# Block-sparse attention with a feed-forward stage: the values of the two end blocks as wide products

## The chip, the core and the metric

The kernel runs on one core of one Trainium2 chip. The core has a matrix engine (TensorE, called PE in the profile; its weight loads are listed apart as PEld), a vector engine (VectorE, DVE), an engine for activation functions (ScalarE, ACT), a general one (GpSimd, POOL) and one that issues transfers (SyncE, SP). Each follows its own list of instructions in order; they wait for one another through semaphores. Matrix products read SBUF and write PSUM. The metric is the time of one execution on the device in microseconds (us). Less is better.

## The reference

The first half is attention for 4 batches and 8 heads, 768 tokens, head size 64. Tokens form 24 blocks of 32. A query block sees itself and its two neighbours, the first and the last block, and three blocks drawn for it; the first and last query blocks see everything. The second half is a feed-forward layer on the 3072 tokens with 512 features, 2048 hidden.

```python
mask = np.abs(blk_i - blk_j) <= window          # window = 1, in blocks of 32
mask = mask | (blk_i == 0) | (blk_j == 0) | (blk_i == n_blocks - 1) | (blk_j == n_blocks - 1)
for qb in range(n_blocks):
    for kb in sampled_blocks[qb]:
        mask[qb * block:(qb + 1) * block, kb * block:(kb + 1) * block] = True
scores = np.where(mask, scale * q @ k.T, -1e9)
attn = softmax(scores);  x = attn @ v           # all heads of a token side by side
out = (gelu(x @ w_in)) @ w_out                  # exact gelu (erf)
```

## The kernel before

The tokens are worked on in nine units of two or three groups (`units`). A group ("quad") is four query blocks, 128 tokens; the first and the last group of a batch have three, because the end query blocks 0 and 23 see everything and are done apart, in "d" rounds. The other groups are made of "s" rounds of two query blocks (one in the second round of a three-block group).

For each s round the kernel does these steps, with the line numbers of the profile:

- `scores` (L305, tile `sc`): products of the queries with eight key blocks for each query block: block 0, the three neighbours, the three drawn ones, block 23. Four heads lie on the four partition quarters, two sets of four heads (G) side by side. Weights are 64 rows by 32 columns.
- `maxima` (L330, tile `nm`, DVE): the negative maximum of each row.
- `exponentials` (L342, tile `pp`, ACT): one exponential of 256 columns for each query block and G. It stores two key blocks interleaved, so that pairs of bf16 can be turned as one 32-bit word. Before the change the blocks 2c and 2c+1 are interleaved.
- `turned` (L359, tile `pT`, DVE): transposes 32x32 words, so that keys lie on partitions. `ptpool` has six such tiles, one for each round.
- `values` (L407, tile `av`), called twice for a group, once for each G ("half"): for each of the eight key blocks c, each query block s and each row half h it makes one product. Weights are the probabilities (64 rows by 32 columns), the moving operand is V with a column of ones, 2 x 65 = 130 columns. The output of query block s goes to partitions 32s to 32s+31, that of row half h to one of two banks.
- `divided` (L422 to L426, DVE) divides by the sum; `outputs` (L436 on PE, tile `tx`, and L444 on ACT, tile `xT`) turns the result for the feed-forward stage.

Where block 0 or 23 is also a neighbour of the query block, it would be counted twice. `values` then takes V from block NB of `kv`, which holds zeros in all its columns, the column of ones included. The same block stands in for drawn blocks that occur twice.

The d rounds use `ptd` (L363) and their values (L383) have weights of 64 x 64.

The feed-forward stage of a unit has `ffn1_step` (L457, tile `hp`, then the gelu of L460) and `ffn2_pieces` (L479, tile `op`), products with 128x128 weights. The order of work is written out by hand (`manual_schedule`): after the first layer of unit n comes `attention` of unit n+1, whose rounds overlap one another, and between their steps PE gets a given number (`quota`) of products of the second layer of unit n as filler. The values of a group are put into PE's list some rounds after the group's last scores, when `due` says so. `psV`, the PSUM pool of `av`, has one buffer.

The lines around the change:

```python
for c in range(8):
    for s, (rnd, i, j) in enumerate(slots):
        ...
        for h in range(2):
            rows = slice(64 * h, 64 * h + 64)
            nc.tensor.matmul(av[32 * s:32 * s + 32, h, V2 * G:V2 * G + V2],
                             lhsT=pv[rows, c // 2, :, c % 2], rhs=src[rows],
                             start=(c == 0), stop=(c == 7))
```

Of the kernel before, what the change touches and what calls it, by code (L numbers as in the profile page):

```python
# [9 lines left out]
F32 = mybir.dt.float32  # L10
BF16 = mybir.dt.bfloat16
I32 = mybir.dt.int32
AF = mybir.ActivationFunctionType
# [6 lines left out]
def kernel(  # L20
# [10 lines left out]
    nc = tc.nc  # L31
    P = 128
    B, H, S, D = q.shape
    assert (B, H, S, D) == (4, 8, 768, 64)
    BL = 32
    NB = S // BL
# [6 lines left out]
    V2 = 2 * VW  # L43
# [13 lines left out]
    ctx.enter_context(tc.manual_schedule())  # L57
    const = ctx.enter_context(tc.tile_pool(name="const", bufs=1))
    ppool = ctx.enter_context(tc.tile_pool(name="ppool", bufs=3))
    ptpool = ctx.enter_context(tc.tile_pool(name="ptpool", bufs=6))  # L60
    small = ctx.enter_context(tc.tile_pool(name="small", bufs=4))
    opool = ctx.enter_context(tc.tile_pool(name="opool", bufs=3))
    psA = ctx.enter_context(tc.tile_pool(name="psA", bufs=2, space=PSUM))
# [17 lines left out]
    g = const.tile([P, KOUT, UT], BF16, name="g")  # L81
# [12 lines left out]
    def sampled(i, r):  # L94
        c0 = GW * (i // 3) + 4 * BW + DW * (i % 3) + BW * r
        return gb[:, c0:c0 + BW]
# [176 lines left out]
    class Unit:  # L273
        def __init__(self, b, quads, dense, i0=0):
# [6 lines left out]
            for grp in self.groups:  # L281
# [4 lines left out]
    units = [Unit(0, (1,), True, 9), Unit(0, (2, 0), False), Unit(0, (3, 4, 5), False)]  # L286
    units += [Unit(b, quads, dense) for b in range(1, B)
              for quads, dense in (((1, 2, 0), True), ((3, 4, 5), False))]
    column = {}
    for n, unit in enumerate(units):  # L290
        for t, quad in enumerate(unit.quads):
# [3 lines left out]
    st = {}  # L295
# [41 lines left out]
    def exponentials(rnd):  # L337
        A, nm = st.pop((rnd, "A")), st.pop((rnd, "nm"))
        pp = ppool.tile([P, 1024], BF16, name="pp")

        def one(dst, src, bias):
            nc.scalar.activation(dst.rearrange("p (c k e) -> p c e k", e=2, k=BL),  # L342
                                 src.rearrange("p (c e k) -> p c e k", e=2, k=BL),
                                 AF.Exp, bias=bias)
        if rnd[0] == "s":
            n = len(rnd[1])
            for x in range(2 * n):
                a = 512 * (x // n) + 256 * (x % n)
                one(pp[:, 256 * x:256 * x + 256], A[:, a:a + 256], nm[:, x:x + 1])
        else:  # L350
            one(pp[:, 0:S], A[:, 0:S], nm[:, 0:1])
        st[rnd, "pp"] = pp

    def turned(rnd):
        pp = st.pop((rnd, "pp"))
        if rnd[0] == "s":
            w = 512 * len(rnd[1])
            pt = ptpool.tile([P, 1024], BF16, name="pT")
            nc.vector.transpose(pt[:, 0:w].bitcast(F32), pp[:, 0:w].bitcast(F32))  # L359
            st[rnd, "pt"] = pt  # L360
        else:
            _, x, G = rnd
            nc.vector.transpose(  # L363
                ptd[:, G].rearrange("p c x q e -> p c (x q e)").bitcast(F32)[:, :, BL * x:BL * x + BL],
                pp[:, 0:S].bitcast(F32).rearrange("p (c k) -> p c k", k=BL))
# [5 lines left out]
    def values(unit, grp, half):  # L371
        kv = kvs[unit.b % 2]
        if half == 0:
            st[grp, "av"] = psV.tile([P, 2, 512], F32, name="av", tag="V")
        av = st[grp, "av"]
        if grp[0][0] == "d":
            pv = ptd.rearrange("p g c x q e -> p g c (x q) e")
            for c in range(NB // 2 * half, NB // 2 * (half + 1)):
                for G in range(2):
                    for h in range(2):  # L380
                        rows = slice(64 * h, 64 * h + 64)
                        c0 = KC + V2 * G
                        nc.tensor.matmul(av[64 * G:64 * G + 64, h, 0:V2],  # L383
                                         lhsT=pv[rows, G, c // 2, :, c % 2],
                                         rhs=kv[rows, c, c0:c0 + V2],
                                         start=(c == 0), stop=(c == NB - 1))
            n, m = 4, 2
        else:
            slots = [(rnd, i, j) for rnd in grp for i, j in enumerate(rnd[1])]
            G = half  # L390
            c0 = KC + V2 * G
            for c in range(8):
                for s, (rnd, i, j) in enumerate(slots):
                    x = len(rnd[1]) * G + i
                    pv = st[rnd, "pt"][:, 256 * x:256 * x + 256]
                    pv = pv.rearrange("p (c k e) -> p c k e", k=BL, e=2)
                    if c in (0, 7):
                        blk = 0 if c == 0 else NB - 1
                        blk = NB if abs(blk - j) <= 1 else blk
                        src = kv[:, blk, c0:c0 + V2]  # L400
                    elif c < 4:
                        src = kv[:, j - 2 + c, c0:c0 + V2]
                    else:
                        src = sampled(unit.place[j], c - 4)[:, c0:c0 + V2]
                    for h in range(2):
                        rows = slice(64 * h, 64 * h + 64)
                        nc.tensor.matmul(av[32 * s:32 * s + 32, h, V2 * G:V2 * G + V2],  # L407
                                         lhsT=pv[rows, c // 2, :, c % 2], rhs=src[rows],
                                         start=(c == 0), stop=(c == 7))
            n, m = len(slots), 4  # L410
            if half:
                for rnd in grp:
                    st.pop((rnd, "pt"))
        if half:
            st[grp, "av"] = av, n, m

# [87 lines left out]
    def attention(unit, filler, quota, tail, held=0, hooks=None, late=False, ahead=None):  # L504
# [17 lines left out]
        def weigh():  # L522
            _, grp, half = due.pop(0)
            values(unit, grp, half)
            if half:
                weighed.append(grp)
# [4 lines left out]
        for it in range(-1, n):  # L531
            last = it + 1 == n
            if not last:
                scores(*rounds[it + 1])
            else:
                while due and due[0][0] <= it:
                    weigh()
            ready = len(given)
            if weighed and not last:
                divide()  # L540
            if it >= 1:
                turned(rounds[it - 1][1])
            if weighed and last:
                divide()
            if not last:
                maxima(rounds[it + 1][1])
            if it >= 0:
                exponentials(rounds[it][1])
            store_finished()
            for f in hooks.get(it, ()):  # L550
                f()
            fill(quota[it + 1])
            if not late:
                store_finished()
            if ready:
                outputs(unit, given.pop(0))
            while not last and due and due[0][0] <= it:
                weigh()
        if not ahead:
            table(AF.Gelu)  # L560
        turned(rounds[n - 1][1])
        for m in tail[:-1]:
            fill(m)
# [54 lines left out]
    for n, unit in enumerate(units):  # L618
        nxt = units[n + 1] if n + 1 < len(units) else None
        b = unit.b  # L620
        fresh = nxt is not None and nxt.b != b
# [91 lines left out]
```

## Time and profile before

| | |
|---|---|
| time, median of 3 runs | 307.44 us (307.2 to 308.11) |
| profiled execution: its time / its span | 308.78 us / 307.0 us |
| busy: PE, PEld, DVE, ACT, POOL | 255.3, 150.1, 219.7, 207.6, 107.9 us |
| value products of s rounds (L407) | 2816, of 218 to 225 ns median each (overlapping) |
| chain that ended last | PE 53%, ACT 17%, DVE 13%, issue 7%, DMA 6% |
| mean granted TensorE clock | 0.972 |

How to read it: a product's duration runs from its start to its modelled end, and products overlap; what one costs in a stream is the distance between starts. Groups are listed as line, engine, operation, output from inputs, shape of the weights (rows * columns), shape of the moving operand, count, then busy time, mean length of one, and the idle time before them with what ended it. In the timeline the first column is the start in us, the second the length; a bracket is idle time before it and what ended it. The chain is followed back from the last instruction to what released each step.

### The profile page before, as it was taken

The page shows a single profiled execution, that of the slowest core. Times are in us where ns is not written, and L with a number is a line of the kernel's source. Part 1 is how long each engine was busy: PE and PEld are TensorE (multiplying, and loading weights), DVE is VectorE, ACT ScalarE, POOL GpSimd, SP SyncE. Part 2 cuts the span into 40 slices and gives each one's busy share as a digit, 9 for nine tenths or more (in the row PEclk, how much of TensorE's full clock was granted, in tenths as well). Part 3 has the DMA queues.
Part 4 walks back from the last instruction along what each step waited for, and adds up shares of the span by engine and source line. Part 5 has one row for each costly group of instructions (what it writes and reads, how often), then busy time and mean ns, then how long its engine had stood idle before and what let it go on. Part 6 is the DMA issues. An engine that isn't in the chain of part 4 may idle for free.

```text
span 307.0 us, 12104 instructions
## 1 busy us (share of the span) xinstructions
PE 255.3 (83%) x5191; PEld 150.1 (49%) x5240; DVE 219.7 (72%) x505; ACT 207.6 (68%) x383; POOL 107.9 (35%) x191
## 2 busy tenths in 40 slices
PE   1656894897589898988799879989998899889994
PEld 0514743653255454534455445635553566355643
DVE  6388675869599895978499876979977979583000
ACT  9666385387476885589367875699668866885621
POOL 8658679987257000567074000500030005000000
PEclk9999996699799999999799999999999999999999
DMA  7999999999949011999699001901000111011001
GB/s 106 157 106 207 207 175 153 210 92 135 116 36 106 3 40 38 190 94 164 75 81 59 15 32 52 204 18 72 5 36 0 38 38 38 0 48 59 3 36 70
DMA packets 90633, 25.44 MB, mean 83 GB/s; under 512 B 81745, under 2 KB 87634, under 8 KB 90578
## 3 DMA queue, kind: packets, MB, share of 16 engines
q0 software_dynamic: 68352, 13.64, 80.8%
q1 hardware_dynamic: 22226, 11.01, 14.3%
q8 instruction: 41, 0.67, 1.0%
q14 instruction: 14, 0.11, 0.2%
HBM read 27.26 MB, written 6.29 MB: 109 GB/s over the span
## 4 chain that ended last, share of the span: by engine, by line
PE 53%; ACT 17%; DVE 13%; issue 7%; DMA 6%; POOL 1%; DVEq 1%; ACTq 0%; POOLq 0%
PE hp L457 24%; PE op L479 12%; PE av L407 9%; ACT pp L342 8%; DVE nm L330 5%; ACT L369 4%; DMA w_in_sb<-in_moe_w_in_dram 3%; ACT g L460 3%; DMA kv<-in_v_dram 2%; PE sc L305 2%; DVE pT L359 2%; PE tx L436 2%; PE av L500 2%; PE op L500 2%; DVE gb L269 2%
## 5 line engine op out<-in xcount | busy, mean ns | idle before, releaser
L342 ACT ACTIVATE pp<-sc,nm 128x256 bf16<-128x256 f32 (+1 forms) x192 | 92.0, 586 | 17.6 <-DVE nm L330 9.2
L457 PE MATMUL hp<-xT,w_in_sb 128*128 128x384 bf16 (+2 forms) x576 | 89.3, 319 | 1.7 <-ACT xT L444 1.3
L479 PE MATMUL op<-w_out_sb,g 128*128 128x512 bf16 x288 | 76.3, 383 | 4.8 <-issue 3.7
L460 ACT ACTIVATE g<-hp 128x768 bf16<-128x768 f32 (+4 forms) x81 | 53.5, 675 | 34.4 <-PE hp L457 34.4
L457 PEld LDWEIGHTS <-w_in_sb 128*128 128x128 bf16 x576 | 56.9, 103 | 34.5 <-issue 4.1
L269 POOL COPY gb<-kv 128x388 bf16 (+1 forms) x69 | 33.3, 530 | 109.0 <-DVE gb L260 83.0
L330 DVE TENSOR_REDUCE nm<-sc 128x4 f32<-128x1024 f32 (+1 forms) x48 | 53.0, 1107 | 7.1 <-PE sc L305 7.0
L269 DVE COPY gb<-kv 128x388 bf16 (+1 forms) x195 | 54.3, 358 | 0.1
L479 PEld LDWEIGHTS <-g 128*128 128x128 bf16 x336 | 28.7, 98 | 36.0 <-issue 12.3
L407 PE MATMUL av<-kv,pT 64*32 64x130 bf16 x1760 | 34.7, 231 | 11.0 <-issue 4.3
L407 PEld LDWEIGHTS <-pT 64*32 64x32 bf16 x2816 | 28.8, 95 | 27.8 <-issue 12.8
L359 DVE STREAM_TRANSPOSE pT<-pp 128x512 f32<-128x512 f32 (+1 forms) x48 | 31.5, 656 | 6.7 <-ACT pp L342 4.5
L444 ACT COPY xT<-tx 128x192 bf16<-128x192 bf16 (+2 forms) x33 | 13.6, 442 | 24.6 <-PE tx L436 24.5
L305 PE MATMUL sc<-gb,qT 64*32 64x256 bf16 x704 | 19.7, 279 | 9.2 <-ACT pp L342 7.8
L305 PEld LDWEIGHTS <-qT 64*32 64x32 bf16 x832 | 12.0, 92 | 29.1 <-issue 23.3
L407 PE MATMUL av<-gb,pT 64*32 64x130 bf16 x1056 | 22.0, 235 | 3.5 <-issue 3.5
L134 POOL DMA_DIRECT2D kv<-in_v_dram x32 | 23.2, 732 | 1.7 <-DMA qn<-in_q_dram 1.1
L369 ACT ACT_TABLE_LOAD x17 | 21.8, 1283 | 0.3
L333 DVE TENSOR_REDUCE nm<-sc 128x1 f32<-128x768 f32 x16 | 15.1, 948 | 9.4 <-PE sc L305 9.1
L422 DVE TENSOR_SCALAR den<-av 128x8 f32<-128x8 f32 (+2 forms) x28 | 4.4, 158 | 21.6 <-PE av L407 21.5
L426 DVE TENSOR_TENSOR xh<-av,rec 128x512 bf16<-128x512 f32 (+2 forms) x28 | 18.2, 652 | 1.0
L465 ACT COPY os<-op 128x512 f32<-128x512 f32 (+1 forms) x23 | 13.1, 569 | 7.3 <-PE op L500 4.2
(64 smaller groups left out, 198.6 us busy)
## 6 DMA issues: line engine op xcount, KB each, us to landing
out_dram<-os SPq DMA_DIRECT2D x23, 256.0 KB, 2.0
kv<-in_v_dram POOLq DMA_DIRECT2D x32, 96.0 KB, 7.6
kn<-in_k_dram POOLq DMA_DIRECT2D x18, 128.0 KB, 8.0
qn<-in_q_dram POOLq DMA_DIRECT2D x18, 128.0 KB, 6.9
w_in_sb<-in_moe_w_in_dram POOLq DMA_DIRECT2D x4, 512.0 KB, 12.9
w_out_sb<-in_moe_w_out_dram POOLq DMA_DIRECT2D x4, 512.0 KB, 17.8
kn<-in_k_dram POOLq DMA_DIRECT2D x2, 384.0 KB, 5.4
qn<-in_q_dram POOLq DMA_DIRECT2D x2, 384.0 KB, 6.8
```

The lines of the kernel that those rows point to most:

```text
L134: nc.gpsimd.dma_start(out=kvs[b % 2][32 * hh:32 * hh + 32, 0:NB, c0:c0 + D], in_=v[b, h].rearrange("(n p) d -> p n d", p=BL))
L269: (engine or nc.vector).tensor_copy(sampled(unit.place[j], r)[:, None, c0:c1], src[:, bass.ds(at[j][r], 1), :])
L305: nc.tensor.matmul(o, lhsT=qT[rows, j // 4, pr, BL * (j % 4):BL * (j % 4) + BL], rhs=rhs(rows, pr), start=True, stop=True)
L330: nc.vector.tensor_reduce(out=nm[:, 0:2 * n].rearrange("p (g j) -> p g j", g=2), in_=A4[:, :, 0:n, :], op=ALU.max, axis=AX.X, negate=True)
L342: nc.scalar.activation(dst.rearrange("p (c k e) -> p c e k", e=2, k=BL), src.rearrange("p (c e k) -> p c e k", e=2, k=BL), AF.Exp, bias=bias)
L359: nc.vector.transpose(pt[:, 0:w].bitcast(F32), pp[:, 0:w].bitcast(F32))
L369: nc.scalar.activation(junk, zero[0:1, 0:1], func)
L407: nc.tensor.matmul(av[32 * s:32 * s + 32, h, V2 * G:V2 * G + V2], lhsT=pv[rows, c // 2, :, c % 2], rhs=src[rows], start=(c == 0), stop=(c ...
L426: nc.vector.tensor_tensor(xh[rows, :, 0:m * D].rearrange("p h (x d) -> p h x d", d=D), a[:, :, :, 0:D], rec[rows, :, 0:m, None].to_broadca ...
L457: nc.tensor.matmul(hp[:, i, 0:T], lhsT=w_in_sb[:, ki, (m + i) * P:(m + i + 1) * P], rhs=xTs[n % 2][:, ki, 0:T], start=(ki == 0), stop=(ki ...
L460: nc.scalar.activation(g[:, m + i[0]:m + i[1], 0:T], hp[:, i[0]:i[1], 0:T], AF.Gelu)
L479: nc.tensor.matmul(op, lhsT=g[:, m, t * P:(t + 1) * P], rhs=w_out_sb[:, m, :], start=(m == 0), stop=(m == KOUT - 1))
```

## The change

Values of a group of four query blocks: the probabilities of all its query blocks now lie in one `pT` tile, `[P, 2, 4, 256]` (G, pair of key blocks, then query block, query, e), filled by the transposes of its two rounds, each at a stride. Key block c is now interleaved with c + 4. The four query blocks' probabilities for one key block are then 128 columns with one step. For blocks 0 and 23, whose V is the same for all four query blocks, `values` makes one product with weights of 64 x 128 in place of four of 64 x 32; these come first in each half. The other six key blocks are done as before. In groups of three the products with the block of zeros are left out. `ptpool` has three buffers of twice the size. `start` and `stop` of the accumulation follow from a list of the work.

```diff
-    ptpool = ctx.enter_context(tc.tile_pool(name="ptpool", bufs=6))
+    ptpool = ctx.enter_context(tc.tile_pool(name="ptpool", bufs=3))
...
+    groups_of = {rnd: grp for unit in units for grp in unit.ends.values() for rnd in grp}
...
         if rnd[0] == "s":
+
             n = len(rnd[1])
             for x in range(2 * n):
                 a = 512 * (x // n) + 256 * (x % n)
-                one(pp[:, 256 * x:256 * x + 256], A[:, a:a + 256], nm[:, x:x + 1])
+                at = pp[:, 0:512 * n].rearrange("p (g c i k e) -> p g i e c k", g=2, c=4, k=BL, e=2)
+                nc.scalar.activation(
+                    at[:, x // n, x % n], A[:, a:a + 256].rearrange("p (e c k) -> p e c k", e=2, k=BL),
+                    AF.Exp, bias=nm[:, x:x + 1])
...
-            w = 512 * len(rnd[1])
-            pt = ptpool.tile([P, 1024], BF16, name="pT")
-            nc.vector.transpose(pt[:, 0:w].bitcast(F32), pp[:, 0:w].bitcast(F32))
-            st[rnd, "pt"] = pt
+            n = len(rnd[1])
+            s = 2 * (rnd != groups_of[rnd][0])
+            if s == 0:
+                st[groups_of[rnd], "pt"] = ptpool.tile([P, 2, 4, 256], BF16, name="pT")
+            pt = st[groups_of[rnd], "pt"]
+            nc.vector.transpose(
+                pt.rearrange("p g c x -> p (g c) x")[:, :, 64 * s:64 * (s + n)].bitcast(F32),
+                pp[:, 0:512 * n].bitcast(F32).rearrange("p (g x) -> p g x", g=8))
...
-            slots = [(rnd, i, j) for rnd in grp for i, j in enumerate(rnd[1])]
+            slots = [j for rnd in grp for j in rnd[1]]
...
+            pv = st[grp, "pt"][:, G].rearrange("p c (q e) -> p c q e", e=2)
+
+            work = []
+            if len(slots) == 4:
+                work += [(0, 4, c, kv[:, blk, c0:c0 + V2]) for c, blk in ((0, 0), (7, NB - 1))]
+            for c in range(1, 7) if work else range(8):
+                for s, j in enumerate(slots):
                     if c in (0, 7):
                         blk = 0 if c == 0 else NB - 1
-                        blk = NB if abs(blk - j) <= 1 else blk
+                        if abs(blk - j) <= 1:
+                            continue
...
+                    work.append((s, 1, c, src))
...
+            for s, w, c, src in work:
...
+                for h in range(2):
+                    rows = slice(64 * h, 64 * h + 64)
+                    nc.tensor.matmul(av[32 * s:32 * (s + w), h, V2 * G:V2 * G + V2],
+                                     lhsT=pv[rows, c % 4, BL * s:BL * (s + w), c // 4], rhs=src[rows],
+                                     start=s in fresh, stop=left[s] == 0)
```

More of the change, by code (lines that the diff above doesn't have):

```diff
@@ L339, in exponentials @@
         pp = ppool.tile([P, 1024], BF16, name="pp")
[L341 to L344, printed above, removed]
         if rnd[0] == "s":
@@ L348, in exponentials @@
                 a = 512 * (x // n) + 256 * (x % n)
-                one(pp[:, 256 * x:256 * x + 256], A[:, a:a + 256], nm[:, x:x + 1])
-        else:
-            one(pp[:, 0:S], A[:, 0:S], nm[:, 0:1])
+                at = pp[:, 0:512 * n].rearrange("p (g c i k e) -> p g i e c k", g=2, c=4, k=BL, e=2)
+                nc.scalar.activation(
+                    at[:, x // n, x % n], A[:, a:a + 256].rearrange("p (e c k) -> p e c k", e=2, k=BL),
+                    AF.Exp, bias=nm[:, x:x + 1])
+        else:
+            nc.scalar.activation(pp[:, 0:S].rearrange("p (c k e) -> p c e k", e=2, k=BL),
+                                 A[:, 0:S].rearrange("p (c e k) -> p c e k", e=2, k=BL),
+                                 AF.Exp, bias=nm[:, 0:1])
         st[rnd, "pp"] = pp
@@ L388, in values @@
         else:
-            slots = [(rnd, i, j) for rnd in grp for i, j in enumerate(rnd[1])]
+            slots = [j for rnd in grp for j in rnd[1]]
             G = half
             c0 = KC + V2 * G
[L392 to L396, printed above, removed]
+            pv = st[grp, "pt"][:, G].rearrange("p c (q e) -> p c q e", e=2)
[4 more added lines that the diff above has]
+                for s, j in enumerate(slots):
                     if c in (0, 7):
                         blk = 0 if c == 0 else NB - 1
-                        blk = NB if abs(blk - j) <= 1 else blk
+                        if abs(blk - j) <= 1:
+                            continue
                         src = kv[:, blk, c0:c0 + V2]
@@ L404, in values @@
                         src = sampled(unit.place[j], c - 4)[:, c0:c0 + V2]
[L405 to L409, printed above, removed]
+                    work.append((s, 1, c, src))
+            fresh, left = set(range(len(slots))), {s: 0 for s in range(len(slots))}
+            for s, w, _, _ in work:
+                for x in range(s, s + w):
+                    left[x] += 1
+            for s, w, c, src in work:
+                at = range(s, s + w)
+                for x in at:
+                    left[x] -= 1
+                for h in range(2):
[3 more added lines that the diff above has]
+                                     start=s in fresh, stop=left[s] == 0)
+                fresh -= set(at)
             n, m = len(slots), 4
             if half:
-                for rnd in grp:
-                    st.pop((rnd, "pt"))
+                st.pop((grp, "pt"))
         if half:
```

## The prediction

> **What bounds the kernel now.** I read the page first (shares, chain, groups), then the stages, the waits, and the timeline around value products.
>
> ```profile
> span 307.0 us, 12104 instructions
> PE 53%; ACT 17%; DVE 13%; issue 7%; DMA 6%; POOL 1%; DVEq 1%; ACTq 0%; POOLq 0%
> ...
> 101.00:122.00 21.00, 18.31 (x589) 10.38 (x594) 16.10 (x30) 15.96 (x36) 0.00 (x0) 1.00 0.08 29
> ...
> 168.50:190.00 21.50, 18.14 (x589) 10.44 (x595) 16.04 (x30) 15.69 (x36) 0.00 (x0) 1.00 0.08 28
> ```
>
> The chain shares say that TensorE (PE) sets most of the time. The two other rows are attention stages (length; then busy time and count for PE, its weight loads, DVE, ACT, POOL): PE is the fullest, so PE time in these stages is what the change has to be priced in. "issue", 7%, is PE ready to go with nothing in the profile to wait for. It needs an explanation before anything else, since the change removes PE instructions:
>
> ```profile
> PE av L407 <- issue: 7.8, 10, 2.2
> PE sc L305 <- issue: 2.2, 2, 1.3
> ...
> 51.87 0.99 issue
> 77.60 2.05 issue
> 83.18 1.29 issue
> 144.74 2.23 issue
> ...
> 144.40 0.34 PE L407 MATMUL av<-gb,pT 64*32 64x130 bf16 x15
> 146.97 0.27 PE L407 MATMUL av<-gb,pT 64*32 64x130 bf16 x9 [2.23 <-issue]
> 146.97 0.15 PEld L407 LDWEIGHTS <-pT 64*32 64x32 bf16 x16 [2.36 <-issue]
> ...
> 79.65:84.45 4.80, 3.53 (x128) 2.03 (x128) 2.37 (x5) 1.62 (x2) 0.00 (x0) 0.64 1.43 90
> 112.10:115.83 3.73, 3.01 (x127) 1.75 (x128) 2.87 (x6) 3.42 (x10) 0.00 (x0) 1.00 0.07 25
> 115.83:119.56 3.73, 3.38 (x127) 2.03 (x128) 1.41 (x4) 1.64 (x2) 0.00 (x0) 1.00 0.15 54
> 180.66:184.39 3.73, 2.87 (x127) 1.76 (x128) 1.67 (x3) 2.10 (x5) 0.00 (x0) 1.00 0.10 37
> 275.77:279.23 3.46, 3.40 (x127) 2.12 (x128) 1.41 (x4) 1.30 (x3) 0.00 (x0) 1.00 0.21 81
> ...
> q8 instruction: 41, 0.67, 1.0%
> ```
>
> First the waits (total, times, longest), then pieces of the chain, then one stall in the timeline: PE stops in the middle of a half of value products, between two of the same kind, both loads and products. 12 such stops come to 10.0 us, on the chain. The windows from one stop's end to the next hold exactly 128 weight loads each time, that is 128 load-product pairs, 256 instructions. Queue q8 (packets, MB, share) brought 0.67 MB in 41 packets, 16 KB each; PE has 5240 pairs, and 10480/41 is 256 again. So PE's instructions come in blocks of 128 pairs, and a block that is used up in less than 3.5 to 3.7 us (the windows without much DMA) makes PE wait for the next. The long stops lie where the DMA engines are loaded (DMA share 1.43 in the window of 4.80 us against 0.07).
> The Trainium skill (Runtime: NRT & Kernel Launch, Instruction fetch mechanics) describes blocks of 16 KiB, 256 instructions, fetched while the current one runs, and calls the crossing mostly hidden. The trace agrees on the block (x128) and not on the hiding (10.0 us); by that page the stops would be something else and would stay, which is rival 1's outcome below.
>
> **The change, part by part.** Counted in the program's order of instructions: each of the 16 four-block groups has two halves of 64 narrow products (64x32 weights); each half becomes 4 wide ones (64x128) and 48 narrow. The 8 three-block groups lose 4 products each. So 544 narrow products go, 128 wide ones come: 4824 pairs instead of 5240.
>
> ```profile
> 206.92 0.81 PE L479 MATMUL op<-w_out_sb,g 128*128 128x512 bf16 x3
> 207.66 0.42 PE L407 MATMUL av<-kv,pT 64*32 64x130 bf16 x32
> ...
> 213.59 0.42 PE L407 MATMUL av<-kv,pT 64*32 64x130 bf16 x32
> 213.85 0.42 PE L407 MATMUL av<-gb,pT 64*32 64x130 bf16 x24
> 214.05 0.28 PE L407 MATMUL av<-kv,pT 64*32 64x130 bf16 x8
> 214.11 0.43 PE L305 MATMUL sc<-kv,qT 64*32 64x512 bf16 x4
> ...
> 106.69 0.88 PE L383 MATMUL av<-kv,ptd 64*64 64x130 bf16 x48 [0.25 <-issue]
> ...
> L407 PEld LDWEIGHTS <-pT 64*32 64x32 bf16 x2816 | 28.8, 95 | 27.8 <-issue 12.8 <-DVE pT L359 8.3 <-DVE xh L426 5.2
> L383 PEld LDWEIGHTS <-ptd 64*64 64x64 bf16 x384 | 7.1, 121 | 2.7 <-issue 1.9 <-DMA w_in_sb<-in_moe_w_in_dram 0.4 <-DVE ptd L363 0.4
> L479 PEld LDWEIGHTS <-g 128*128 128x128 bf16 x336 | 28.7, 98 | 36.0 <-issue 12.3
> ```
>
> **Products removed.** A half of 64 narrow products starts at 213.59 and the next work at 214.11: 0.52 us, 8.1 ns each. That is the first point against the change: eight narrow products (four blocks, two row halves) run side by side and cost together 65 ns. 544 x 8.1 ns = -4.4 us.
> **Products added.** 48 products of 64x64 take 0.88 us, of which the last alone 0.22: 0.66/11 = 60 ns for each four, which are two column halves by two row halves. A wide product fills all columns, so two (the row halves) go side by side; 64 such pairs at 60 ns are +3.8 us. Whether their weights load in time is unknown: the load rows grow by 26 ns from 32 to 64 columns, so 128 columns could need 121 + 52 = 173 ns, or 98 like the full 128x128. Taken: hidden, since the loads of 121 ns are hidden at 60 ns a step; the other end is 113 ns exposed for each of 64 pairs, 7.2 us more.
> **Changes of tile shape.** Three op products start 0.215 apart ((0.81-0.38)/2, the last at 207.35), but the first narrow product comes at 207.66, 0.31 later: 0.095 us for going from 128x128 to 64x32. The wide products stand first in each half, so 32 times PE goes from 64x128 to 64x32, and 7 or so times back to wide from narrow: 149 changes of shape in the program become 188, 39 more. No row shows 64x128 against 64x32, where only the columns differ; the ends are 0 and 0.095 us. I take 0.095, the only measured change of shape: +3.7 us.
> The Trainium skill (TensorEngine Tiling, Key Properties) says that changing the tiling mode, not just the tile, drains the engine. By that rule all 39 cost (+3.7 us), and the product arithmetic alone turns from -0.6 to a loss; no run here shows it for this pair of shapes yet.
> **Sum on the array:** -4.4 + 3.8 + 3.7 = +3.1 us. In two units of nine the first group's values lie beside a chain of ACT and DVE (4 halves of 32 hidden), so +2.7 on the path. Ends: -0.5 with free changes of shape, +9 with exposed loads.
>
> **Fetch.** A half gets 12 pairs shorter. An attention stage takes 21.0/594 = 35 ns for a pair on the mean; a block with two halves in it therefore reaches 24 pairs further, 24 x 35 ns = 0.85 us, and its two halves take 2 x 3.1/32 = 0.2 us longer: the block lasts about 1.0 us more before the next is needed. The nine stops of 0.99 us and less (10.0 - 2.05 - 1.29 - 2.23 = 4.4 us) would go, the three long ones lose 1.0 each: 7.4 us. But ACT and DVE work on during a stop; where PE no longer stops it meets their transposes earlier:
>
> ```profile
> PEld L407 <- DVE pT L359: 8.3, 17, 1.6
> PE av L407 <- DVE xh L426: 4.0, 2, 2.3
> ```
>
> These waits (for the probabilities, and for the single value bank to be read) are what is late next; they already stand in 19 places. I count 0.7 of the gain: -5.2 us. Ends: 0 (the block borders move into other dense spots) and -7.4.
>
> **Edits at no cost.** The transpose now writes runs at a stride:
>
> ```profile
> L359 DVE STREAM_TRANSPOSE pT<-pp 128x512 f32<-128x512 f32 x40 | 28.0, 700 | 6.7 <-ACT pp L342 4.5 <-issue 2.0
> L363 DVE STREAM_TRANSPOSE ptd<-pp 128x384 f32<-128x384 f32 x16 | 9.1, 568 | 3.2 <-ACT pp L342 3.2
> L359 DVE STREAM_TRANSPOSE pT<-pp 128x256 f32<-128x256 f32 x8 | 3.5, 433 | 0.0
> L342 ACT ACTIVATE pp<-sc,nm 128x256 bf16<-128x256 f32 x176 | 74.9, 539 | 9.5 <-DVE nm L330 9.2
> ```
>
> The 384 form already writes with a stride and its 568 ns lies midway between 433 and 700 (566.5), so the stride is free. The exponentials write the same runs of 32 at the same step, only to other places; I take 539 ns unchanged (10 ns each would be 1.8 us on ACT, a quarter of it on the chain, 0.4 us). Three pT buffers of double size hold what six held, and the order shows the transposes waiting on ACT alone, as before. A half's first product now needs both rounds' transposes where the first four narrow ones needed one: 4 x 8.1 ns, nothing. DVE, POOL and SP keep their order.
>
> **Sum.** +2.7 - 5.2 = -2.5 us. The profiled execution took 308.78 us (span 307.0 and 1.78 around it), so 306.3 for it; it lay 1.34 above the median of 307.44, which I carry to 304.9. This kernel's runs cannot tell less than about 0.3% (0.9 us) from nothing.
>
> **Rivals.** 1, slower: the array pays for the changes of shape in each half, and the stops do not shrink, because the block borders fall into other dense spots (8% fewer blocks, but each still meets two halves). For it, a whole block used in 1.13 us where two halves follow each other:
>
> ```profile
> 245.54 1.13 PEld L407 LDWEIGHTS <-pT 64*32 64x32 bf16 x128 [0.42 <-DVE pT L359]
> ```
>
> Against: 12 pairs less in each half, and most halves stand apart. Price +2.7: 310.1; with weight loads exposed more. It decides as soon as the fetch gain on the path is under 1.8 us. 2, changes of shape are free where the rows stay 64: -0.5 instead of +2.7, time 307.44 - 0.5 - 5.2 = 301.7. Against it stands the row of 0.31. 3, no difference: half of the fetch gain (2.6) against 2.7 on the array, 307.4; for it speak the waits on DVE above, which could take the place of the stops.
>
> **Chances.** Forecast (302.5 to 306.5) 0.46; rival 2 (below 302.5) 0.14; rival 3 0.12, a sixth of it just faster; rival 1 0.28. Faster 0.62, same 0.10, slower 0.28. The range 301.0 to 310.3 leaves out half of rival 2's lower tail and the part of rival 1 with exposed loads; the forecast's own range is 302.5 to 306.5.
>
> **What would show it.** Wide products in pairs about 60 ns apart at the head of each half, then a gap of some 0.15 us before the narrow ones (60 and 95); without the gap rival 2 holds. The waits "av <- issue" and "sc <- issue" together near 3 us instead of 10.0, and windows of 128 loads that last over 3.7 us without a stop; if they stay at 10, rival 1. The transposes at 700 and 433 ns, the exponentials at 539. The prediction falls if the wide loads take 170 ns and show before each second pair, or if waits on DVE grow by as much as the stops shrink.

## The result and the profile after

The changed kernel takes 306.46 us (median of 20 runs) against 308.06 us for the kernel before in as many runs of the same sessions. The ratio is 0.9941, with a 95% interval of 0.9915 to 0.9967: 1.8 us less, between 1.0 and 2.6. A later, separate comparison gave 0.990 (0.9836 to 0.9964); executions over 1.5% above the fastest of their kernel are left out of such ratios, there seven of the changed kernel's twelve. The profiled execution has a span of 305.9 us.

The page of the changed kernel: the span, the packets of PE's instruction queue, the chain.

```profile
span 305.9 us, 11321 instructions
...
q8 instruction: 38, 0.62, 0.9%
...
PE 62%; ACT 17%; DVE 8%; DMA 6%; issue 4%; POOL 1%; DVEq 1%; POOLq 0%; ACTq 0%
```

"issue" went from 7% to 4% of the span, three packets of 16 KB fewer were fetched, and PE's share of the chain rose from 53% to 62%. PE's busy time, 255.3 us before and 265.1 us after, can't be compared: the first trace lacks the records of 48 op products (before, then after):

```profile
L479 PE MATMUL op<-w_out_sb,g 128*128 128x512 bf16 x288 | 76.3, 383 | 4.8 <-issue 3.7
...
L498 PE MATMUL op<-w_out_sb,g 128*128 128x512 bf16 x336 | 87.6, 387 | 0.2
```

The 11.3 us between the two rows are more than the whole difference in busy time, and the 3.7 us of "issue" in the first row (0.2 us of idle time in the second) are gaps where records are missing, not stops. PE's waits say more (total us, times, longest; the first row is the kernel before):

```profile
PE av L407 <- DVE pT L359: 2.6, 5, 1.5
...
PEld L426 <- DVE pT L365: 14.1, 20, 3.2
...
PE av L426 <- DVE pT L365: 5.7, 4, 2.9
PE av L426 <- issue: 4.9, 4, 2.1
PE av L426 <- DVE xh L445: 1.9, 2, 1.3
PE tx L455 <- issue: 0.9, 2, 0.7
...
149.32:153.32 4.00, 3.75 (x128) 2.08 (x128) 3.27 (x9) 1.25 (x2) 0.00 (x0) 1.00 0.22 60
```

The stops in the middle of work were 10.0 us before in two rows, with one of 0.25 us (at 74.10) that isn't at the border of a block: 290 loads lie between it and the stop before it. That leaves 11 stops of 9.7 us. Now they are 4.9 us in the row of the value products and 0.9 us in that of `tx`, whose two stops lie at borders as well: the one at 54.41 us comes after 732 loads, as the first stop before did, and the one at 153.33 us 128 loads behind that at 149.32 (last row). So 9.7 us became 5.9 us, in 6 stops. A second profile of the changed kernel has 4.5 us of them (4.4 in the value products, 0.2 in `tx`).

The wait of the value products for the transposes has grown, from 2.6 to 5.7 us on PE and from 8.3 to 14.1 us on its weight loads (the two rows overlap in part and can't be added). Their wait for the single value bank (`xh`) fell from 4.0 to 1.9 us, so that the two together went from 6.6 to 7.6 us. At the first group, waits of 2.31 us for the bank and 0.32 us for a transpose became one of 2.93 us for a transpose.

What a half now looks like, in the timeline and by shapes:

```profile
111.89 0.38 PE L498 MATMUL op<-w_out_sb,g 128*128 128x512 bf16 x1
112.20 0.29 PE L426 MATMUL av<-kv,pT 64*128 64x130 bf16 x4
...
112.42 0.36 PE L426 MATMUL av<-kv,pT 64*32 64x130 bf16 x24
112.60 0.42 PE L426 MATMUL av<-gb,pT 64*32 64x130 bf16 x24
112.80 0.44 PE L306 MATMUL sc<-gb,qT 64*32 64x256 bf16 x16
...
L426 PEld LDWEIGHTS <-pT 64*128 64x128 bf16 x128 | 3.7, 96 | 15.4 <-DVE pT L365 11.5 <-issue 3.0
L365 DVE STREAM_TRANSPOSE pT<-pp 128x512 f32<-128x512 f32 x40 | 28.0, 701 | 6.8 <-ACT pp L348 4.6 <-issue 2.0
L365 DVE STREAM_TRANSPOSE pT<-pp 128x256 f32<-128x256 f32 x8 | 3.5, 433 | 0.0
L348 ACT ACTIVATE pp<-sc,nm 128x256 bf16<-128x256 f32 x176 | 75.1, 542 | 11.2 <-DVE nm L331 11.0
```

The four wide products take 0.29 us including the last one's own 0.22, so the second pair starts 0.07 us after the first. The first narrow product comes at 112.42, 0.22 us after the half's start: two pairs at 0.065 us and 0.09 us more for the change from 64x128 to 64x32. The whole half lasts 0.60 us (112.20 to 112.80), 0.08 us longer than the 0.52 before, for 52 pairs in place of 64. The wide weights load in 96 ns, against 95 for the narrow ones before, and nothing shows before the second pair.

Three attention stages of the program are alike (615 load-product pairs before, 563 after) and run at a granted clock of 1.00. The rows show them from the last product of one first layer to the first of the next, then two halves of values that follow each other in the third, first of the kernel before, then of the changed one:

```profile
99.05:122.06 23.01, 19.80 (x607) 11.03 (x616) 17.81 (x33) 17.92 (x38) 0.00 (x0) 1.00 0.10 27
166.39:189.94 23.55, 19.67 (x608) 11.09 (x616) 17.61 (x32) 17.68 (x38) 0.00 (x0) 1.00 0.09 26
230.59:252.10 21.51, 19.21 (x607) 10.98 (x615) 17.53 (x31) 17.69 (x38) 0.00 (x0) 1.00 0.08 27
245.54:246.74 1.20, 1.20 (x129) 1.13 (x128) 0.98 (x2) 1.09 (x3) 0.00 (x0) 1.00 0.06 14
...
101.84:123.80 21.96, 20.98 (x563) 10.94 (x563) 17.53 (x31) 17.79 (x38) 0.00 (x0) 1.00 0.08 27
166.12:188.11 21.99, 21.05 (x562) 10.98 (x563) 17.53 (x31) 17.75 (x38) 0.00 (x0) 1.00 0.16 28
229.57:251.41 21.84, 20.89 (x562) 10.92 (x563) 17.54 (x31) 17.74 (x38) 0.00 (x0) 1.00 0.08 28
244.56:246.07 1.51, 1.51 (x106) 1.16 (x105) 1.13 (x2) 1.41 (x3) 0.00 (x0) 1.00 0.00 0
```

Here both sides of the change can be seen apart. The third stage has no stop in either kernel and got 0.33 us longer, for four halves: the price of the array. The first two had three stops of 1.06 us and two of 1.57 us before, and none of 0.1 us or more now; they got 1.05 and 1.56 us shorter. Before, they were 1.50 and 2.04 us longer than the third, so a stop cost more than the idle time that the rows of waits count: the two halves that take 1.20 us in the third stage took 2.12 us in the first, with one stop counted as 0.55 us.

### The profile page after: what moved, and what is told of

The parts are those of the page before. It is cut to its first block, busy times and chain, and to the rows that moved or that the text cites. A ratio compares the mean times of both kernels' runs of the same rounds, so it can differ in the third digit from the quotient of the medians.

```text
span 305.9 us, 11321 instructions
## 1 busy us (share of the span) xinstructions
PE 265.1 (87%) x4824; PEld 149.6 (49%) x4824; DVE 219.5 (72%) x505; ACT 208.0 (68%) x383; POOL 109.9 (36%) x191
## 4 chain that ended last, share of the span: by engine, by line
PE 62%; ACT 17%; DVE 8%; DMA 6%; issue 4%; POOL 1%; DVEq 1%; POOLq 0%; ACTq 0%
PE hp L476 26%; PE op L498 15%; PE av L426 11%; ACT pp L348 7%; ACT L376 4%; DMA w_in_sb<-in_moe_w_in_dram 3%; PE sc L306 3%; ACT g L479 3%; PE tx L455 3%; DMA kv<-in_v_dram 2%; DVE nm L331 2%; PE av L519 2%; DVE pT L365 2%; PE op L519 2%; DVE xh L445 1%
## 5 line engine op out<-in xcount | busy, mean ns | idle before, releaser
L498 PE MATMUL op<-w_out_sb,g 128*128 128x512 bf16 x336 | 87.6, 387 | 0.2
L348 ACT ACTIVATE pp<-sc,nm 128x256 bf16<-128x256 f32 x176 | 75.1, 542 | 11.2 <-DVE nm L331 11.0
L269 DVE COPY gb<-kv 128x388 bf16 (+1 forms) x195 | 52.9, 352 | 0.1
L426 PEld LDWEIGHTS <-pT 64*32 64x32 bf16 (+1 forms) x2400 | 28.0, 97 | 30.5 <-DVE pT L365 14.1
L426 PE MATMUL av<-kv,pT 64*32 64x130 bf16 (+1 forms) x1344 | 30.4, 232 | 8.2 <-DVE pT L365 5.7
L352 ACT ACTIVATE pp<-sc,nm 128x768 bf16<-128x768 f32 x16 | 17.1, 1100 | 10.4 <-DVE nm L334 10.4
```

The lines of the kernel that those rows point to most:

```text
L269: (engine or nc.vector).tensor_copy(sampled(unit.place[j], r)[:, None, c0:c1], src[:, bass.ds(at[j][r], 1), :])
L348: nc.scalar.activation(at[:, x // n, x % n], A[:, a:a + 256].rearrange("p (e c k) -> p e c k", e=2, k=BL), AF.Exp, bias=nm[:, x:x + 1])
L426: nc.tensor.matmul(av[32 * s:32 * (s + w), h, V2 * G:V2 * G + V2], lhsT=pv[rows, c % 4, BL * s:BL * (s + w), c // 4], rhs=src[rows], start ...
L498: nc.tensor.matmul(op, lhsT=g[:, m, t * P:(t + 1) * P], rhs=w_out_sb[:, m, :], start=(m == 0), stop=(m == KOUT - 1))
```

## The experiments

The theory: the change costs PE time in each half (wide products and changes of tile shape) and saves more than that by stopping less often for the next block of 128 load-product pairs. The rivals: the gain comes from the layout alone; changes of shape are free; the stops are not caused by the use of blocks. All ratios are to the kernel before on the same chip.

### The layout alone

All values narrow as before (no group has five query blocks), in the new layout, zero products still dropped.

```diff
-            if len(slots) == 4:
+            if len(slots) == 5:
                 work += [(0, 4, c, kv[:, blk, c0:c0 + V2]) for c, blk in ((0, 0), (7, NB - 1))]
```

> The changed layout and the dropped zero products, but all values narrow: 5208 pairs, 39 changes of tile shape fewer than in the changed kernel. Theory (the time is array cost against stops for the next block of 128 pairs): the layout costs nothing, 32 products fewer save 0.3 us, the stops stay near 10 us; 307.5 us where the kernel before takes 307.9, ratio 0.996 to 1.002. Rival (the layout or the shared tile made the gain): ratio 0.994 as for the change.

Measured: 0.9993 (0.9961 to 1.0024). The stops in its profile, and the loads counted from one stop's end to the next:

```profile
PE av L426 <- issue: 7.4, 10, 2.7
...
PE sc L306 <- issue: 0.8, 1, 0.8
...
113.74:117.47 3.73, 3.02 (x127) 1.78 (x128) 2.87 (x6) 2.97 (x7) 0.00 (x0) 1.00 0.09 32
270.90:274.63 3.73, 3.05 (x127) 1.83 (x128) 2.09 (x4) 2.21 (x6) 0.00 (x0) 1.00 0.04 15
```

The layout and the dropped zeros are worth nothing that can be measured. The gain needs the wide products: the two ratios lie 0.0052 apart, 1.6 us, known to about 1.3 us either way. The stops have moved to other places and come to 8.0 us with 10 of them (the two rows, less one of 0.25 us that isn't at a border), not quite the 10 us expected, but their spacing of 128 loads and 3.73 us is the one of the kernel before.

### One of the two wide products at the end of the half

```diff
                     work.append((s, 1, c, src))
+            if len(slots) == 4:
+                work.append(work.pop(1))
```

> As the changed kernel, with the wide product of block 23 moved from the head to the end of its half: the same 4824 pairs, 47 more changes of tile shape. Theory (each change of shape costs 0.09 us): 47 x 0.09 = 4.2 us on PE, 0.88 of it on the path, 3.7 us: 309.9 us, ratio 1.006. Rival (a change between 64x128 and 64x32 is free and the gap of 147 ns behind the wide products is something else, such as their weight loads): no difference to the changed kernel, ratio 0.994.

Measured: 1.0041 (1.0006 to 1.0077), 0.010 above the changed kernel's 0.9941, 3.1 us. The products and the instruction count are the same; only their order differs. A half of this kernel in the timeline:

```profile
110.01 0.53 PE L428 MATMUL av<-kv,pT 64*128 64x130 bf16 x26
110.35 0.42 PE L428 MATMUL av<-gb,pT 64*32 64x130 bf16 x24
110.71 0.23 PE L428 MATMUL av<-kv,pT 64*128 64x130 bf16 x2
110.87 0.41 PE L306 MATMUL sc<-gb,qT 64*32 64x256 bf16 x16
```

The first row holds the wide pair at the head and 24 narrow products behind it. The wide pair at the end starts at 110.71, and the scores, narrow again, 0.16 us later: 0.065 us for a pair and some 0.09 us for the change of shape. The same 0.16 us stand ahead of the wide pair: the last of the narrow products starts at 110.55 (the row's end, less the 0.22 us of that product). In both places the weight loads pause too, for 0.07 us up to 110.70 and up to 110.87, so the gap isn't time spent on loading, and the rival that changes between 64x128 and 64x32 are free falls. 47 more of them at 0.09 us are 4.2 us on PE; 3.1 us arrived, and the stops in this profile were 3.7 us, fewer than the changed kernel's. The two halves that follow each other in the stage without stops show the price undisturbed:

```profile
243.12:244.74 1.62, 1.62 (x105) 1.24 (x105) 1.13 (x2) 1.52 (x3) 0.00 (x0) 1.00 0.07 28
```

They take 1.62 us here with one change of shape more than in the changed kernel, which takes 1.51.

### Op products split in two

```diff
-                nc.tensor.matmul(op, lhsT=g[:, m, t * P:(t + 1) * P], rhs=w_out_sb[:, m, :],
-                                 start=(m == 0), stop=(m == KOUT - 1))
+                for i in range(2):
+                    cs = slice(256 * i, 256 * i + 256)
+                    nc.tensor.matmul(op[:, cs], lhsT=g[:, m, t * P:(t + 1) * P],
+                                     rhs=w_out_sb[:, m, cs],
+                                     start=(m == 0 and i == 0), stop=(m == KOUT - 1 and i == 1))
```

> As the changed kernel, with each op product of 512 columns made as two of 256: 336 more pairs, nothing else. Array: two of 256 take some 0.005 us more than one of 512, 336 x 0.005 = 1.7 us, 1.5 on the path. Theory (blocks of 128 pairs): blocks in the attention stages are used up sooner, the stops grow from 4.9 to about 9 us; together +4.5 us, 310.7 us, ratio 1.009, and 128 loads between stops as before. Rival (the stops have another cause): only the array's part, 307.7 us, ratio 0.999, stops near 5 us.

Measured: 1.0043 (1.0006 to 1.0081), 3.1 us above the changed kernel. Here are the group of op products of this kernel, its stops, and one window between two stops:

```profile
L500 PE MATMUL op<-w_out_sb,g 128*128 128x256 bf16 x672 | 87.8, 276 | 0.2
...
PE av L426 <- issue: 7.6, 7, 1.9
...
144.44:150.45 6.01, 4.47 (x127) 3.15 (x128) 3.83 (x7) 3.05 (x6) 0.39 (x1) 1.00 1.70 144
```

The split costs the array next to nothing (87.8 us busy for 672 products, against 87.6 us for 336 in the changed kernel), less than the 1.7 us expected. The stops grow to 7.6 us, from 5.9 us in one profile of the changed kernel and 4.5 in the other, 1.7 to 3.1 us of the 3.1, and again 128 loads lie between them. So pairs that cost hardly any array time cost time all the same, and the rival's ratio of 0.999 lies outside the interval; the expected 9 us of stops and the ratio of 1.009 were too much.

### The products of the end blocks left out

This kernel leaves out the values of blocks 0 and 23 for the groups of four, so its time is that of less work.

```diff
-            if len(slots) == 4:
-                work += [(0, 4, c, kv[:, blk, c0:c0 + V2]) for c, blk in ((0, 0), (7, NB - 1))]
-            for c in range(1, 7) if work else range(8):
+            for c in range(1, 7) if len(slots) == 4 else range(8):
```

> As the changed kernel, without the wide products: the values of blocks 0 and 23 are left out for the groups of four, 4696 pairs, 39 changes of tile shape fewer. Theory: 64 wide pairs at 0.064 us and 39 changes at 0.09 us go, 7.6 us on PE, 0.88 of it on the path, 6.7 us: 299.5 us where the kernel before takes 307.8, ratio 0.973. If the time that PE saves comes back as waits on the transposes, up to 303. Rival (wide products and changes of shape lie beside other work or cost nothing): ratio 0.992 to 0.994.

Measured: 0.9758 (0.9693 to 0.9823), 5.6 us below the changed kernel where 6.7 were expected (ratio 0.973), within the interval. Wide products and their changes of shape, 7.6 us on PE by the theory, are paid for the most part. The run can't price them alone, since its waits on issue differ too:

```profile
PE sc L306 <- issue: 4.2, 1, 4.2
...
PE av L424 <- issue: 3.4, 4, 1.5
```

They are 7.6 us here, more than in the changed kernel, though there are fewer pairs. The two halves that follow each other are free of them:

```profile
237.11:238.05 0.94, 0.94 (x97) 0.87 (x97) 0.86 (x2) 0.83 (x2) 0.00 (x0) 1.00 0.00 0
```

0.57 us less than the changed kernel's 1.51, for four wide pairs and three changes of shape: 0.53 us by the theory.

### Fewer transfers

This kernel leaves out the loads of keys and queries for batches 1 and 2; these batches work on old data. PE's instructions are the same.

```diff
-                    load_kq_by_token(1)
+                    for x in (kn, qn):
+                        nc.gpsimd.memset(by_token(x)[96:128], 0.0)
...
-                    load_kq_by_token(2)
```

> As the changed kernel, without the loads of keys and queries for batches 1 and 2 (two small fills of the tiles' unused rows in their place, so batches 1 and 2 work on old data). The same instructions on PE. Theory (a stop lasts longer where the transfers delay PE's next block): the stops near 77, 84 and 149 us, 1.5, 2.1 and 0.9 us in the changed kernel, become 0 to 0.7 us each; the later ones stay. Rival (they are long for another reason, such as a wait on data): they stay as they are. Time 302 to 305 us by the theory, ratio 0.98 to 0.99.

Measured: 0.9789 (0.9733 to 0.9846). The same window of the changed kernel (first row) and of this one (second fence); the last three columns are the granted clock, the DMA share as the view gives it, and GB/s:

```profile
76.50:84.00 7.50, 4.87 (x154) 2.44 (x158) 3.83 (x7) 4.12 (x8) 2.72 (x4) 0.76 2.33 165
```

```profile
76.50:84.00 7.50, 5.06 (x253) 3.10 (x242) 7.17 (x14) 5.48 (x12) 0.00 (x0) 1.00 0.02 4
...
PE av L426 <- issue: 1.2, 3, 0.6
```

Without the transfers no stop is left near 77 and 84 us, and the one near 149 us is 0.6: 1.2 us of stops in place of 5.9 (4.5 in the second profile). In the changed kernel the two early stops lie exactly one block apart, with the DMA engines loaded:

```profile
76.82:83.66 6.84, 4.54 (x127) 2.12 (x128) 3.83 (x7) 3.80 (x7) 2.62 (x3) 0.75 2.38 158
```

128 loads in 6.84 us, where blocks came in 3.7 with hardly any transfers: the block arrives later while the transfers run. A wait on the loaded data would have gone with them as well; against it stand the 128 loads and that the profile names no such wait there. The time fell by 4.7 us from the changed kernel's, a little more than expected (0.9789 for 0.98 to 0.99). How much of that is the stops, this run can't tell, since it also takes away waits on the loads themselves, and the granted clock was higher.

### The wide products of both halves together

The wide products of both halves are made at the head of the first half, so that the second has none.

```diff
-            if len(slots) == 4:
-                work += [(0, 4, c, kv[:, blk, c0:c0 + V2]) for c, blk in ((0, 0), (7, NB - 1))]
-            for c in range(1, 7) if work else range(8):
+            four = len(slots) == 4
+            if four and half == 0:
+                for GG in range(2):
+                    cc = KC + V2 * GG
+                    pw = st[grp, "pt"][:, GG].rearrange("p c (q e) -> p c q e", e=2)
+                    for c, blk in ((0, 0), (7, NB - 1)):
+                        for h in range(2):
+                            rows = slice(64 * h, 64 * h + 64)
+                            nc.tensor.matmul(av[:, h, V2 * GG:V2 * GG + V2],
+                                             lhsT=pw[rows, c % 4, :, c // 4],
+                                             rhs=kv[rows, blk, cc:cc + V2],
+                                             start=c == 0 and GG == 0, stop=False)
+            for c in range(1, 7) if four else range(8):
...
-                                     start=s in fresh, stop=left[s] == 0)
+                                     start=s in fresh, stop=left[s] == 0 and (half == 1 or not four))
```

(For groups of four `fresh` starts empty.) It was run three times, the last time beside the changed kernel on one chip.

> As the changed kernel, with the wide products of both halves of a group made at the head of its first half: 4824 pairs, 22 changes of tile shape fewer. Theory: 22 x 0.09 = 2.0 us less on PE, 1.7 on the path: 304.5 us, ratio 0.989. If the time saved comes back as waits on the transposes or as earlier stops, between 304.5 and 306.2. Rival (changes of shape are free): ratio 0.994.

> The wide products of both halves at the head of the first half once more, to narrow its interval against the changed kernel's 0.994: between 0.989 (all 2.0 us of 22 changes of shape on the path) and 0.994 (none).

> The changed kernel itself, on the same chip as the next one: ratio 0.994 to the kernel before (0.9915 to 0.9967).

> The wide products of both halves at the head of the first half, beside the changed kernel: 22 changes of tile shape fewer, 0.3 to 0.6% below it (ratio 0.988 to 0.991) if they lie on the path, no difference if the waits on the transposes take them back.

Measured: 0.9924 (0.9894 to 0.9953), 0.9891 (0.9855 to 0.9927), 0.9918 (0.9886 to 0.9951); the changed kernel beside the last 0.990 (0.9836 to 0.9964). It beats the kernel before each time, by 0.8 to 1.1%. Against the changed kernel it lies 0.2 to 0.5% lower in the first two runs and 0.2% higher in the direct comparison, whose interval is wide (the medians of all twelve executions there, 304.2 us against 305.5 for the changed kernel, point the other way). The times alone leave open whether 22 changes of shape less are worth anything on the path. The two halves that follow each other settle it for their place:

```profile
240.80:242.07 1.27, 1.27 (x105) 1.10 (x105) 1.04 (x2) 1.16 (x4) 0.00 (x0) 1.00 0.00 0
```

They take 1.27 us, 0.24 less than in the changed kernel, for the same products and two changes of shape fewer. Their whole stage takes 21.59 us here, and 21.59 and 21.58 in the other two profiles, against 21.84 and 21.83 in the two of the changed kernel, so there the saving is on the path. With 0.94 us without wide products, 1.20 with narrow ones only, 1.51 in the changed kernel and 1.62 with one change more, a change of shape in the middle of the values costs 0.11 to 0.12 us; four wide pairs and a single change (1.27) cost 0.07 us more than the 32 narrow products they replace (1.20).

## Why the prediction was right, point by point

**The sum.** Forecast were 304.9 us, 2.5 us less than before. The kernel became 1.8 us faster (1.0 to 2.6). The time of 306.46 us lies inside the range, at the upper edge of the forecast's own range, in part because the kernel before took 308.06 us in these sessions, not 307.44.

**The array.** The prices were 60 ns for a wide pair, 95 ns for a change of shape, and hidden weight loads. Measured were 65 ns, 90 to 120 ns, and 96 ns loads that show nowhere. The change between 64x128 and 64x32, which no row of the kernel before showed, is there in all 32 halves, and the kernel with 47 more such changes is slower by 3.1 us. That was the step with ends of 0 and 0.095 us; the upper end was right, and the Trainium skill's rule (TensorEngine Tiling, Key Properties) that a change of mode drains the engine agrees with these 90 to 120 ns. The trace's order of weight loads has 162 changes before and 201 after, where the prediction counted 149 and 188: the 39 more, on which the term rests, are the same. With wide pairs at 65 ns the products alone save 0.2 us (4.4 less 4.2), not 0.6. The forecast of +2.7 us on the path holds: four halves cost 0.33 us in the stage without stops, which makes 2.6 us for 32, an estimate from that stage. So the array alone would have lost time, and the gain comes from the stops, as the three like stages show directly.

**The fetch.** The mechanism was right and the size of this term was not: the stops were to fall by 7.4 us before the factor of 0.7, and they fell by 3.8 us (9.7 to 5.9), or 5.2 us by the second profile. Of the nine short ones, one was no stop at a border; of the other eight, 4.1 us in all, three of 0.26 to 0.69 us are left, 1.4 us. The three long ones, which were to lose 1.0 us each and keep 2.6 us in all, did not: 1.49, 2.06 and 0.95 us were left, 4.5 us in all (4.4 in the second profile). The step that failed is that a block that lasts longer shortens a long stop by as much. Under transfers the next block comes later, by an amount that changes from stop to stop (6.84 us for one block, against 3.7), as the run with fewer loads shows. The Trainium skill (Runtime: NRT & Kernel Launch, Instruction fetch mechanics) calls the crossing of a block mostly hidden; with 128 loads between stops in four kernels, and stops that follow the number of pairs, the trace stands against that for this stream of short products.

**The part of the gain that counts.** 0.7 of it was taken, because transposes would be late next. PE's wait for them did rise by 3.1 us, but its wait for the value bank fell by 2.1, so that only 1.0 us of the gain can have gone this way. With 2.6 us for the array, 3.8 to 5.2 us of stops saved would leave 1.2 to 2.6 us if all of it counts and 0.1 to 1.0 us if 0.7 does; 1.8 (1.0 to 2.6) were measured. That speaks for nearly all, but sums over one profiled execution are a rough measure beside a median: the two profiles of the changed kernel have spans of 305.9 and 303.0 us, and a stop costs more than the idle time counted for it. The factor is not settled. That 0.7 of 7.4 us came near the truth is in part luck, since too large a fall was multiplied by a share that the waits don't bear out.

**The edits at no cost.** Transposes took 701 and 433 ns (700 and 433 before), exponentials 542 (539 before), and the layout alone changed nothing (0.9993).

**The rivals.** That the stops do not shrink fell with 9.7 to 5.9 us, though they did not come down to the 3 us named as the sign. That changes of shape are free fell with the wide product moved to the end. That nothing would come of it lies outside the interval, which ends at 0.9967, and the waits of the value products on DVE grew by 1.0 us, not by as much as the stops shrank.

## What to carry to other kernels

Count instructions on PE as well as array time: where this kernel used 128 pairs of weight load and product in less than about 3.7 us, the next block was late, and fewer, larger products gained although the array did no less. Small products that already run side by side in the array cost little each: sixteen narrow ones cost 0.13 us here (8.1 ns each), as much as the two wide pairs in their place (65 ns each), and every change of tile shape of 90 to 120 ns came on top. Idle time that the profile gives to "issue" in the middle of a stream is worth counting: equal numbers of weight loads between the stops told what it was. Before summing such gaps, look whether the trace has all records of the engine: a missing product looks like idle time too.

## What the runs showed of the hardware that was not expected

Stops and a lower clock went together in one place: in the window from 76.5 to 84 us the granted TensorE clock was 0.76 in the changed kernel, with stops of 1.5 and 2.1 us, and 1.00 in the kernel with fewer loads and none there. That the stops caused it was not tried, and stops alone don't bring it: the kernel with split op products stopped for 1.57, 1.54 and 0.72 us between 142 and 155 us at a granted clock of 1.00. And PE's instruction packets are slowed by the kernel's own transfers: with a DMA load of 0.02 in place of 2.33 in that window the stops there vanished, with the same instructions.
